# Part B of a two-branch attention kernel: dense Q, K and output projections, heads laid out through DRAM, and a queue order written by hand

## The chip, the cores and the metric

The kernel runs as one program on one core of a Trainium2 chip. The metric is the device time of one execution in microseconds, compared as the median of several runs. The engines named below are PE (matrix multiplication, with its weight loads PEld), ACT (ScalarE), DVE (VectorE), POOL (GpSimd) and SP (SyncE, which here only issues DMAs). ACT issues DMAs too, on a queue of its own.

## What is computed

Two attention branches read the same x (2048 tokens of 640) and are mixed by a gate.

```python
g = sigmoid((x * gate_w).sum(-1))
# A: 64 segments of 32 tokens; 8 memory rows are carried from segment to segment
h = concat(mem, x_segment)                       # 40 rows
q, k, v = h @ Wq, h @ Wk, h @ Wv                 # 32 heads of 192
o = softmax(mask(q k^T * 192**-0.5)) v @ Wo;  mem = o[:8];  a = o[8:]
# B: 32 heads of 20; each token sees itself and 7 earlier tokens, 2 apart
q, k, v = split(x @ wqkv)
b = softmax(q . k[t - 2w], w = 0..7) v[t - 2w] @ wo
out = g * a + (1 - g) * b
```

All tensors are bf16. The program does branch B first, then a prepass that projects the x rows which share a tile with memory rows, then the 64 segments of branch A in a recurrence, then a last stage.

## The kernel before

Branch B is the function `part_b`. It takes the 2048 tokens in blocks of 484 (four full blocks, b = 0 to 3, and a last one of 112), and the 32 heads in 8 groups of four (g = 0 to 7). One pair (b, g) is a step; there are 40.

Four heads of a group lie 32 rows apart, so that four small matmuls can sit in the four 32-row strips of PE. A head has 20 rows only. The weights of Q and K (`wqk`, names wq_pad and wk_pad) are therefore copied into tiles with 32 columns a head, of which 12 are zero, and the output weights (`wop`, name wo_pad) are loaded by four DMAs into 20 of each 32 partitions.

The pieces of part B, with their lines in the profile:

- `make_xT(b)` transposes 512 tokens of x into `xT` (L164), loads the next x tiles on ACT's queue (L118), computes the gate (L175 to L181), and on POOL packs rows for branch A (L185 to L190); SP stores them in `xh_dram` (L187).
- `make_v(b)` projects V for four sets of 128 keys (L213).
- `proj(b, g)` projects Q and K of one group of heads from the padded weights (L226), five matmuls each; DVE copies Q to SBUF, ACT copies K (helper lines L79 and L77).
- `scores(b, g)` has two halves of two heads each. Each half is 8 matmuls (L244), an exponential on ACT (L249, tile bP) and a multiplication by the band mask on DVE (L253).
- `values(b, g)` is called a step later. It multiplies bP by ones (sum, ps_bZ) and by V (ps_bO), 16 matmuls each in turn (L266); ACT takes logarithm and exponential for the reciprocal (L271, L272), and DVE writes the product to `OT` (L274), which is laid out like the padded heads.
- `out_tile(ti)` multiplies 128 tokens of `OT` by wo_pad, 8 terms for each of two halves (L282); ACT and DVE scale by 1 - g (L285, L287) and ACT's queue stores to `bsc_dram` (L289).

PSUM has two buffers for projections, transposes, V and output, two pairs for scores, and one each for sum and value. The steps are written in the order of the loop below, but the order of the instructions on each engine is chosen by a planner that moves instructions by their priority.

```python
for i, (b, g) in enumerate(steps):
    if g == 2 and b + 1 < S // 512: make_xT(b + 1)
    if g == 6 and i + 8 < len(steps): make_v(b + 1)
    if i + 1 < len(steps): proj(*steps[i + 1])
    scores(b, g)
    if i > 0: values(*steps[i - 1])
    if g >= 1 and b > 0 and 128 * (ti + 1) <= BQ * b: out_tile(ti); ti += 1
```

Beside part B the weights of branch A are loaded. They are cut into 80 slices of 384 KB. `load_early` (after the first xh store) loads 23 of them (N_EARLY) to stay in SBUF, and copies all 20 slices of Wo in DRAM into `wscr`, where a partition's part is contiguous (L385). 27 more (`late[0]`) are loaded when part B gives its SBUF free, others in the prepass and after it. Fourteen slices do not stay and are streamed once a segment (tile wst). The prepass projects Q, K (L442) and V (L454) and is held until the first xh store; the segment loop and the last stage are `part_a` and `part_z` (L569 and on).

Of the kernel before, what the change touches and what calls it, by code (L numbers as in the profile page):

```python
# [15 lines left out]
N_EARLY = 23  # L16
# [11 lines left out]
class _K:  # L28
# [61 lines left out]
    def part_b(self):  # L90
# [3 lines left out]
        BQ = 4 * NQ  # L94
        scale_b = 20.0 ** (-0.5)
# [6 lines left out]
        with ExitStack() as ctx:  # L102
# [13 lines left out]
            def load_x(i):  # L116
                xs[i] = io.tile([128, 640], BF, name="x_sb")
                nc.scalar.dma_start(xs[i][:], self.x2d[i * 128:(i + 1) * 128, :])  # L118
# [5 lines left out]
            wop = wp.tile([128, 8, 640], BF, name="wo_pad")  # L124
            wqk = [wp.tile([128, KC, 32, 32], BF, name=f"w{n}_pad") for n in "qk"]
            xT = wp.tile([128, KC, HALO + S], BF, name="xT")
            OT = wp.tile([128, 8, S], BF, name="OT")
            wsrc = self.wqkv.rearrange("(c p) f -> p c f", p=128)
            for n, w in enumerate(wqk):
                nc.gpsimd.memset(w[:, :, :, 20:32], 0.0)  # L130
                raw = OT[:].rearrange("p g t -> p (g t)")[:, 3200 * n:3200 * n + 3200]
                (nc.scalar, nc.sync)[n].dma_start(raw.rearrange("p (c f) -> p c f", c=KC), wsrc[:, :, 640 * n:640 * n + 640])
                for kc in range(KC):
                    eng = (nc.vector, nc.gpsimd)[(KC * n + kc) % 2]
                    eng.tensor_copy(w[:, kc, :, 0:20], raw[:, 640 * kc:640 * kc + 640].rearrange("p (h d) -> p h d", d=20))
            nc.sync.dma_start(gw[:], self.gate_w.rearrange("(c p o) -> p c o", p=128, o=1))
            nc.scalar.dma_start(wv[:], wsrc[:, :, 1280:1920])
            nc.gpsimd.memset(wop[:], 0.0)
            wosrc = self.wo.rearrange("(g h d) f -> h d g f", h=4, d=20)
            for hh in range(4):  # L140
                nc.sync.dma_start(wop[32 * hh:32 * hh + 20, :, :], wosrc[hh])
# [14 lines left out]
            self.g_sb = wp.tile([128, self.NT], F32, name="g_sb")  # L156
            self.omg_sb = wp.tile([128, self.NT], F32, name="omg_sb")

            def make_xT(b):
                t0 = 512 * b  # L160
                for kc in range(KC):
                    ps = bank(BF, "ps_xT")
                    for i in range(4):
                        nc.tensor.transpose(ps[:, i * 128:(i + 1) * 128], xs[4 * b + i][:, kc * 128:(kc + 1) * 128],  # L164
                                            self.ident[:])
                    self.evac(xT[:, kc, HALO + t0:HALO + t0 + 512], ps[:, 0:512])
# [5 lines left out]
                for i in range(4):  # L172
                    c0 = HALO + t0 + 128 * i
                    for kc in range(KC):
# [5 lines left out]
                nc.vector.reciprocal(self.g_sb[:, gs], gz[:, gs])  # L180
                nc.vector.tensor_scalar(out=self.omg_sb[:, gs], in0=self.g_sb[:, gs], scalar1=-1.0, scalar2=1.0,  # L181
# [5 lines left out]
                xh_store = nc.sync.dma_start(self.xh_dram[16 * b:16 * b + 16].rearrange("s p f -> p s f"),  # L187
                                    xh[:].rearrange("p s c t -> p s (c t)"))
                self.first_store = self.first_store or xh_store.ins
# [13 lines left out]
            def make_v(b):  # L203
                nq, nu, c0 = shape_of(b)
                nk = nq + 7
                for u in range(nu):
                    V = wk.tile([128, 652], BF, name=f"bV{u}")
                    nc.vector.memset(V[:, 640:652], 0.0)
                    k0 = c0 + 242 * (u // 2) + u % 2
                    for f in range(2):  # L210
                        ps = bank(F32, "ps_bv")
                        for kc in range(KC):
                            nc.tensor.matmul(ps[0:nk, 0:320], lhsT=xT[:, kc, k0:k0 + 2 * nk - 1:2],  # L213
                                             rhs=wv[:, kc, 320 * f:320 * f + 320], start=(kc == 0), stop=(kc == KC - 1))
                        self.evac(V[0:nk, 320 * f:320 * f + 320], ps[0:nk, 0:320])
                    Vs[b, u] = V

            qk = {}

            def proj(b, g):  # L220
                nq, nu, c0 = shape_of(b)
                nt = nq * nu
                for n, (o0, nn) in enumerate(((c0 + HALO, nt), (c0, nt + HALO))):
                    ps = bank(F32, "ps_bqk")
                    for kc in range(KC):
                        nc.tensor.matmul(ps[:, 0:nn], lhsT=wqk[n][:, kc, 4 * g:4 * g + 4, :].rearrange("p h d -> p (h d)"),  # L226
                                         rhs=xT[:, kc, o0:o0 + nn], start=(kc == 0), stop=(kc == KC - 1))
                    t = wk.tile([128, BQ + HALO], BF, name="b" + "qk"[n] + "T", bufs=3)
                    self.evac(t[:, 0:nn], ps[:, 0:nn], "dve" if n == 0 else "act")
                    qk[b, g, n] = t  # L230
# [3 lines left out]
            def scores(b, g):  # L234
# [61 lines left out]
            make_xT(0)  # L296
            with tc.issue_after(self.first_store):
                self.load_early()
            make_v(0)
            proj(*steps[0])  # L300
            ti = 0
            for i, (b, g) in enumerate(steps):
# [648 lines left out]
```

## Time and profile before

| | us |
|---|---|
| median of 3 runs | 1759.83 (1757.96 to 1762.52) |
| the profiled execution, its own time | 1748.09 |
| its span, first to last instruction | 1746.1 |
| part B with its start | 0 to 225.4 |
| prepass | 225.4 to 384.5 |
| 64 segments of branch A | 384.5 to 1687.2 |
| last stage | 1687.2 to 1746.1 |

Over the span PE is busy 1666.4 us (95%), ACT 868.5, DVE 649.4 and POOL 69.9. The granted clock of PE is 0.998. In a row of a profile, "L226 PE MATMUL ps_bqk<-xT,wk_pad 128*128 128x498 bf16 x160 | 38.8, 372 | 1.7 <-ACT" reads: line 226 of the kernel, engine and operation, output and inputs, shape, how many; busy time in us and mean ns of one; the idle time of the engine ahead of them, and what ended it. Matmuls are pipelined, so the mean of one is longer than the distance from one to the next.

### The profile page before, as it was taken

Reading aid. Unit: us, or ns where it says so; the run is one execution under the profiler, and the core shown is the slowest. Engines: PE = TensorE matmul, PEld = TensorE weight load, DVE = VectorE, ACT = ScalarE, POOL = GpSimd, SP = SyncE. Lnnn points to the kernel's source line nnn. Section 1 sums busy time; section 2 is a strip of 40 time slices with the busy share of each in tenths; the row PEclk is TensorE's granted clock in tenths of the full one; section 3 lists DMA queues with packets and bytes.
Section 4 is the critical chain, followed back from the end, with each engine's and each line's share of the span. In section 5 each row is a group of like instructions: output and inputs, shape, how many; then the busy total and the mean of one; then the engine's idle time right before and its main releaser. Section 6 shows DMA issues by size and latency. Waiting matters only on the chain.

```text
span 1746.1 us, 82407 instructions
## 1 busy us (share of the span) xinstructions
PE 1666.4 (95%) x36527; PEld 994.9 (57%) x36527; DVE 649.4 (37%) x2065; ACT 868.5 (50%) x2377; POOL 69.9 (4%) x132
## 2 busy tenths in 40 slices
PE   6899999999999999999999999999999999999989
PEld 3555544445556555556555555555555555555557
DVE  4565533223333333333333333333333333333330
ACT  3776632224555555555555555555555545555550
POOL 4011000000000000000000000000000000000000
PEclk9999999999999999999999999999999999999999
DMA  6951184899999999999999999999999989999981
GB/s 172 335 133 27 42 303 113 221 275 309 307 299 304 298 309 299 305 301 308 295 302 302 299 300 300 302 298 307 303 297 305 298 295 300 306 302 298 300 288 30
DMA packets 280648, 466.50 MB, mean 267 GB/s; under 512 B 94820, under 2 KB 155748, under 8 KB 280292
## 3 DMA queue, kind: packets, MB, share of 16 engines
q1 hardware_dynamic: 178632, 401.83, 69.6%
q10 hardware_dynamic: 101660, 59.41, 11.7%
q8 instruction: 285, 4.67, 1.1%
q14 instruction: 71, 0.58, 0.1%
HBM read 427.47 MB, written 41.55 MB: 269 GB/s over the span
## 4 chain that ended last, share of the span: by engine, by line
PE 86%; ACT 7%; issue 2%; DMA 2%; DVE 2%; ACTq 1%; DVEq 0%
PE ps_qk L569 26%; PE ps_v L662 13%; PE ps_wo L726 12%; PE ps_qkT L586 6%; PE ps_pre L442 6%; PE ps_S L616 5%; PE ps_oT L685 3%; PE ps_z L883 3%; PE ps_bqk L226 3%; ACT bP L249 2%; PE ps_pre L454 2%; ACT ZB L810 2%; PE ps_mem L736 1%; PE ps_bv L213 1%; PE ps_S L625 1%
## 5 line engine op out<-in xcount | busy, mean ns | idle before, releaser
L578 ACT CAST TZ<-ps_qk 128x384 bf16<-128x384 f32 x448 | 208.2, 479 | 326.2 <-PE ps_qk L569 180.4
L569 PEld LDWEIGHTS <-hT 128*32 128x32 bf16 x10240 | 246.5, 96 | 150.0 <-DVE hT L739 13.2
L593 DVE COPY ZB<-ps_qkT 128x384 bf16<-128x384 bf16 x256 | 91.6, 358 | 377.6 <-PE ps_qkT L586 211.7
L569 PE MATMUL ps_qk<-wres_q,hT 128*32 128x384 bf16 x4096 | 225.8, 327 | 1.8 <-issue 1.5
L662 PE MATMUL ps_v<-wlate_v,hT 128*32 128x384 bf16 x4096 | 224.6, 329 | 0.0
L726 PEld LDWEIGHTS <-TZ 128*32 128x32 bf16 x6144 | 153.6, 96 | 65.8 <-issue 18.0
L569 PE MATMUL ps_qk<-wlate_k,hT 128*32 128x384 bf16 x2560 | 159.7, 328 | 0.0
L569 PE MATMUL ps_qk<-wst,hT 128*32 128x384 bf16 x1792 | 153.2, 328 | 0.3 <-issue 0.2
L662 PEld LDWEIGHTS <-hT 128*32 128x32 bf16 x5120 | 113.6, 96 | 68.9 <-issue 6.2
L726 PE MATMUL ps_wo<-wlate_oa,TZ 128*32 128x384 bf16 x2560 | 139.2, 327 | 2.3 <-issue 2.3
L616 PE MATMUL ps_S<-ZB,TZ 128*128 128x160 bf16 (+1 forms) x1024 | 136.9, 238 | 0.4 <-issue 0.4
L586 PE MATMUL ps_qkT<-ident,TZ 128*128 128x128 bf16 x1536 | 130.2, 221 | 0.2 <-issue 0.2
L726 PE MATMUL ps_wo<-wlate_ob,TZ 128*32 128x256 bf16 x2688 | 123.2, 275 | 7.4 <-issue 7.3
L586 PEld LDWEIGHTS <-TZ 128*128 128x128 bf16 x1536 | 89.1, 98 | 61.3 <-issue 40.8
L569 PE MATMUL ps_qk<-wres_k,hT 128*32 128x384 bf16 x1792 | 120.3, 328 | 1.2 <-issue 0.6
L634 ACT ACTIVATE ZB<-ps_S 32x224 bf16<-32x224 f32 x256 | 89.0, 348 | 41.7 <-PE ps_S L625 38.1
L696 DVE CAST TZ<-ps_oT 128x192 bf16<-128x192 f32 x256 | 79.4, 351 | 63.6 <-PE ps_oT L690 63.6
L696 ACT CAST TZ<-ps_oT 128x192 bf16<-128x192 f32 x256 | 69.7, 327 | 57.7 <-PE ps_oT L690 57.7
L616 PEld LDWEIGHTS <-TZ 128*128 128x128 bf16 (+1 forms) x1024 | 58.9, 95 | 68.4 <-issue 41.0
L739 DVE CAST hT<-ps_mem 128x24 bf16<-128x24 f32 x126 | 22.6, 179 | 195.7 <-PE ps_mem L736 195.7
L669 ACT CAST TZ<-ps_v 128x384 bf16<-128x384 f32 x192 | 92.3, 481 | 3.2
L546 POOL COPY TZ<-ZB 128x384 bf16<-128x384 bf16 x64 | 32.5, 507 | 1495.9 <-DMA ZB<-zpk_dram 582.5
(142 smaller groups left out, 2431.2 us busy)
## 6 DMA issues: line engine op xcount, KB each, us to landing
wst<-in_A_Wq_dram SPq DMA_DIRECT2D x260, 384.0 KB
wst<-in_A_Wv_dram SPq DMA_DIRECT2D x260, 384.0 KB
wst<-in_A_Wk_dram SPq DMA_DIRECT2D x195, 384.0 KB
wst<-wscr SPq DMA_DIRECT2D x192, 384.0 KB
zpk_dram<-ZS ACTq DMA_DIRECT2D x4, 3072.0 KB
ZB<-zpk_dram ACTq DMA_DIRECT2D x64, 192.0 KB
wscr<-in_A_Wo_dram SPq DMA_DIRECT2D x20, 384.0 KB
wres_q<-in_A_Wq_dram SPq DMA_DIRECT2D x16, 384.0 KB
```

The costliest lines, as they stand in the source:

```text
L226: nc.tensor.matmul(ps[:, 0:nn], lhsT=wqk[n][:, kc, 4 * g:4 * g + 4, :].rearrange("p h d -> p (h d)"), rhs=xT[:, kc, o0:o0 + nn], start=(kc ...
L442: nc.tensor.matmul(ps[:], lhsT=sls[r][kc][:, c0:c0 + 128], rhs=zTi[:, kc, :], start=(kc == 0), stop=(kc == KC - 1))
L569: nc.tensor.matmul(pq[32 * j:32 * j + 32, 0:384], lhsT=hT[:, kc, :], rhs=sl[:, 384 * j:384 * j + 384], start=(kc == 0), stop=(kc == KC - 1 ...
L578: cp(sts[i], pqs[i][:, 0:384])
L586: nc.tensor.transpose(pT[:, t, :, :, :].rearrange("p j b i -> p (j b i)"), st[:, 128 * t:128 * t + 128], self.ident[:])
L593: nc.vector.tensor_copy(q_blocks(R)[:, 1:5, :, :].rearrange("p b c i -> p c b i"), pT.rearrange("p t j b i -> p (t j) b i"))
L616: nc.tensor.matmul(grid(h, par)[:, :, 0:80].rearrange("p j (b r i) -> p j b r i", r=2, i=8)[:, :, :, r, :], lhsT=KT[k0:k1, 12 * r + c:12 * ...
L634: nc.scalar.activation(E[ps], pSs[h][ps, :, 112 * j:112 * j + 112], ACT.Exp, scale=scale_a)
L662: nc.tensor.matmul(pvs[R][32 * j:32 * j + 32, 0:384], lhsT=hT[:, kc, :], rhs=sl[:, 384 * j:384 * j + 384], start=(kc == 0), stop=(kc == KC ...
L669: cp(V[R], pvs[R][:, 0:384])
L696: cps[j % 2](oTxs[2 * h + j // 2][:, 6 * (j % 2):6 * (j % 2) + 6, :], pos[j][:, 0:240].rearrange("p (c q) -> p c q", q=40)[:, :, 8:40])
L726: nc.tensor.matmul(pso[part][32 * jj:32 * jj + 32, 0:n], lhsT=oTxs[2 * (R // 2) + j // 2][:, 6 * (j % 2) + 3 * (R % 2) + t, :], rhs=o_weig ...
```

## The change

Q and K are projected densely, in five chunks of 128 columns a block instead of eight groups of four padded heads, and the output projection has five terms instead of eight. The rows of the heads are put 32 apart by DMA: each chunk is copied to a staging tile (`bqkD`, four buffers), stored in DRAM, and read back by halves of 16 heads into `bqkT`, four DMAs of 20 partitions each (`load_qk`). The normalized output goes the same way back: four DMAs of 20 partitions store it by halves in DRAM, and one loads it densely into `OT` (`load_o`). This is done a block ahead: while block b is attended, block b + 1 is projected.

The order on PE, ACT, DVE and SP is written out by hand (`manual_schedule`); each step has scores, the values of the step before, and a list of jobs. In `values` all 16 sums come before all 16 products. The last, short block is attended in two steps of 16 heads instead of eight of four. One early slice is loaded a step, 20 in all (N_EARLY), and only seven slices of Wo are copied to `wscr`; the other thirteen are read from Wo itself. The stores to `bsc_dram` go to SP's queue. The prepass is held until the output of block 2 is reloaded (`mid_load`). The zero padding, its memsets and copies are gone.

```diff
-N_EARLY = 23
+N_EARLY = 20
...
-                nc.scalar.dma_start(xs[i][:], self.x2d[i * 128:(i + 1) * 128, :])
+                eng = nc.sync if i < 2 else nc.scalar
+                eng.dma_start(xs[i][:], self.x2d[i * 128:(i + 1) * 128, :])
...
-            wop = wp.tile([128, 8, 640], BF, name="wo_pad")
-            wqk = [wp.tile([128, KC, 32, 32], BF, name=f"w{n}_pad") for n in "qk"]
+            wo = wp.tile([128, KC, 640], BF, name="b_wo")
+            wqk = [wp.tile([128, KC, 640], BF, name=f"b_w{n}") for n in "qk"]
...
-            OT = wp.tile([128, 8, S], BF, name="OT")
+            OT = wp.tile([128, KC, S], BF, name="OT")
...
-            for n, w in enumerate(wqk):
-                nc.gpsimd.memset(w[:, :, :, 20:32], 0.0)
...
-                    eng.tensor_copy(w[:, kc, :, 0:20], raw[:, 640 * kc:640 * kc + 640].rearrange("p (h d) -> p h d", d=20))
+            nc.sync.dma_start(wqk[0][:], wsrc[:, :, 0:640])
+            nc.scalar.dma_start(wqk[1][:], wsrc[:, :, 640:1280])
+            nc.sync.dma_start(wv[:], wsrc[:, :, 1280:1920])
...
+            def proj(b, f, n):
...
+                if n == 0:
+                    qk["D"] = wk.tile([128, 2, BQ + HALO], BF, name="bqkD", bufs=4)
+                t = qk["D"]
+                ps = bank(F32, "ps_bqk")
+                for kc in range(KC):
+                    nc.tensor.matmul(ps[:, 0:nn], lhsT=wqk[n][:, kc, 128 * f:128 * f + 128], rhs=xT[:, kc, c0:c0 + nn],
+                                     start=(kc == 0), stop=(kc == KC - 1))
+                self.evac(t[:, n, 0:nn], ps[:, 0:nn], "dve" if n == 0 else "act")
+                if n == 1:
+                    for half in range(2):
...
+                            nc.sync.dma_start(qk_dram[b][half, :, r0 - 320 * half:r1 - 320 * half, :].rearrange("n p x -> p n x"),
+                                              t[r0 - 128 * f:r1 - 128 * f, :, 0:nn])
+            def load_qk(b, half):
...
+                t = wk.tile([128, 2, 4, BQ + HALO], BF, name="bqkT", bufs=3)
+                src = qk_dram[b][half].rearrange("n (g h d) x -> h d (n g) x", h=4, d=20)
+                for hh in range(4):
+                    nc.sync.dma_start(t[32 * hh:32 * hh + 20, :, :, 0:nn].rearrange("p n g x -> p (n g) x"), src[hh])
...
+                if gs[-1] % 4 == 3:
+                    g = gs[-1]
+                    for hh in range(4):
+                        nc.sync.dma_start(heads(ot_dram[b][:])[hh][:, g - 3:g + 1, :], oT[32 * hh:32 * hh + 20, :, 0:nt])
+            def load_o(b):
...
+                load = nc.sync.dma_start(OT[:, :, BQ * b:BQ * b + nt], ot_dram[b][:].rearrange("(c p) n -> p c n", p=128))
+                if b == 2:
+                    self.mid_load = load.ins
...
+                for c in range(KC):
+                    nc.tensor.matmul(ps[:, 0:320], lhsT=OT[:, c, 128 * ti:128 * ti + 128],
+                                     rhs=wo[:, c, 320 * f:320 * f + 320], start=(c == 0), stop=(c == KC - 1))
...
+                for i, (b, gs) in enumerate(steps):
+                    g, nb, jobs = gs[0], b + 1, []
+                    if nb < NB:
+                        nu = shape_of(nb)[1]
+                        if g == 0 and nb < S // 512:
+                            jobs += [lambda kc=kc: xT_chain(nb, kc) for kc in range(KC)] + [lambda: gate(nb)]
+                        chunk = {1: 0, 2: 1, 3: 2, 5: 3, 6: 4}.get(g)
+                        if chunk is not None:
+                            jobs += [lambda n=n: proj(nb, chunk, n) for n in range(2)]
+                        vs = {1: (0,), 2: (1,), 3: (2,), 4: (3, 4), 7: (5, 6, 7)}.get(g, ())
+                        jobs += [lambda u=u: v_chain(nb, u // 2, u % 2) for u in vs if u < 2 * nu]
+                        for _ in range({0: 1, 4: 2, 5: 1, 6: 1, 7: 2}.get(g, 0) if b < NB - 2 else 1):
+                            if outs:
+                                jobs.append(outs.pop(0))
...
+                    scores(b, gs, 0)
+                    scores(b, gs, 1)
+                    if prev:
+                        values(*prev)
+                    mask(b, gs, 0)
+                    if jobs:
+                        jobs.pop(0)()
+                    mask(b, gs, 1)
+                    if prev:
+                        recip(*prev)
+                    if jobs:
+                        jobs.pop(0)()
+                    if prev:
+                        norm(*prev)
+                    for job in jobs:
+                        job()
...
+                    if nb < NB and g == 4:
+                        load_qk(nb, 0)
+                    if nb < NB and g == 7:
+                        load_qk(nb, 1)
+                    if g == 1 and b > 0:
+                        add_outs(b - 1)
+                    if early:
+                        early.pop(0)()
...
-        so = [k for k in self.slice_keys() if k[0] in ("oa", "ob") and k not in self.early]
+        so = [k for k in self.slice_keys() if k[0] in ("oa", "ob") and (k in self.stream_keys or k in self.late[3])]
...
-        with tc.issue_after(k.first_store):
+        with tc.issue_after(k.mid_load):
             k.prepass()
```

310 lines of the change are left out of this document (179 added, 131 removed).

## The prediction

> **What bounds the kernel now.** First the busy time of each engine in the stretches of the program (columns: stretch, its length, busy time of PE, PEld, DVE, ACT and POOL with instruction counts, granted clock, DMA share, GB/s): part B with start, then prepass, segment loop and last rows.
>
> ```profile
> 0.00:225.40 225.40, 193.27 (x2724) 113.79 (x2724) 124.46 (x251) 138.80 (x249) 37.49 (x68) 0.99 0.46 138
> 225.40:384.50 159.10, 156.22 (x724) 70.42 (x728) 47.98 (x71) 40.57 (x72) 0.51 (x1) 1.00 0.78 234
> 384.50:1687.20 1302.70, 1264.23 (x31540) 766.65 (x31543) 469.20 (x1730) 677.85 (x2048) 31.95 (x63) 1.00 0.92 302
> 1687.20:1746.10 58.90, 52.73 (x1552) 44.00 (x1544) 7.75 (x15) 11.28 (x10) 0.00 (x0) 1.00 0.26 76
> ```
>
> PE fills the prepass and the segment loop, and the change leaves their arithmetic alone. What it can win lies in the first 225.4 us. The same view by block of part B (start, blocks 0 to 3, short block 4):
>
> ```profile
> 0.00:31.40 31.40, 17.62 (x100) 10.09 (x100) 13.12 (x36) 5.49 (x10) 16.41 (x19) 0.95 0.66 184
> 31.40:64.20 32.80, 30.82 (x455) 16.98 (x454) 19.76 (x36) 24.69 (x40) 3.66 (x3) 1.00 0.81 293
> 64.20:111.00 46.80, 41.09 (x593) 23.84 (x592) 25.68 (x49) 31.56 (x52) 4.25 (x3) 1.00 0.93 258
> 111.00:158.00 47.00, 42.56 (x606) 25.13 (x606) 27.62 (x50) 30.80 (x51) 13.17 (x43) 1.00 0.12 31
> 158.00:198.00 40.00, 35.69 (x518) 20.20 (x520) 23.09 (x39) 27.33 (x45) 0.00 (x0) 1.00 0.09 28
> 198.00:225.40 27.40, 25.50 (x464) 17.56 (x464) 15.19 (x44) 18.93 (x56) 0.00 (x0) 1.00 0.11 40
> ```
>
> A full block takes 47 us: PE 41 to 43, ACT 31. PE is the bound, ACT has a third to spare. Which PE work, by groups with shapes apart, over part B:
>
> ```profile
> L249 ACT ACTIVATE bP<-ps_bS 128x968 bf16<-128x968 f32 x64 | 59.5, 984 | 0.1
> L226 PE MATMUL ps_bqk<-xT,wk_pad 128*128 128x498 bf16 x160 | 38.8, 372 | 1.7 <-ACT gz_sb L178 1.7
> L282 PE MATMUL ps_bo<-wo_pad,OT 128*128 128x320 bf16 x256 | 38.7, 300 | 0.7 <-DVE bqT L79 0.7
> L226 PE MATMUL ps_bqk<-xT,wq_pad 128*128 128x484 bf16 x160 | 38.0, 367 | 4.6 <-ACT bo L285 4.5
> L213 PE MATMUL ps_bv<-wv_sb,xT 128*128 128x320 bf16 x160 | 27.3, 331 | 4.7 <-DVE bV L79 3.3 <-ACT bV L77 1.4
> ```
>
> Then one step without extra work, in the timeline: ACT runs from the two exponentials through logarithm and reciprocal to the next K copy without a gap, so beneath PE's load ACT is the second bound.
>
> ```profile
> 68.75 1.85 ACT L249 ACTIVATE bP<-ps_bS 128x968 bf16<-128x968 f32 x2
> 70.48 0.59 ACT L271 ACTIVATE b_rz<-ps_bZ 128x484 f32<-128x484 f32 x1
> 71.11 0.61 ACT L272 ACTIVATE b_rz<-b_rz 128x484 f32<-128x484 f32 x1
> 71.62 0.57 ACT L77 CAST bkT<-ps_bqk 128x498 bf16<-128x498 f32 x1
> ```
>
> Last, what DMA moves of the kinds that the change adds: 23 to 25 us is the padded Wo load (DMAs of 20 partitions), 26 to 28 the xh store (320 B runs), 45 to 60 slices in 3 KB rows, 70 to 80 mostly the Wo copies in 768 B rows.
>
> ```profile
> 23.00:25.00 2.00, 2.00 (x10) 1.09 (x9) 0.49 (x1) 0.00 (x0) 0.17 (x1) 0.50 0.69 123
> 26.00:28.00 2.00, 2.00 (x14) 1.14 (x12) 0.69 (x2) 0.42 (x1) 0.61 (x2) 0.94 1.08 210
> 45.00:60.00 15.00, 13.86 (x194) 8.08 (x191) 8.96 (x16) 11.13 (x19) 0.00 (x0) 1.00 1.03 404
> 70.00:80.00 10.00, 8.76 (x161) 5.75 (x160) 6.90 (x15) 8.79 (x14) 0.46 (x1) 1.00 0.98 291
> ```
>
> **PE per block.** Prices from the chain of waits: 20 projection matmuls in 4.21 us (0.21 each), 30 V matmuls in 4.36 (0.145), 16 output matmuls in 2.17 to 2.33 (0.14); scores plus values of a step take 0.91 to 1.15 in the timeline, say 1.0. A full block now: 80 projections 16.8, V 5.8, 64 output 9.0, eight steps 8, transposes and gate about 2: 41.6, against 41.1 read. After: dense Q and K need 5 chunks of 128 columns instead of 8 groups, 50 matmuls of 498 (10.5); output 5 terms instead of 8, 40 matmuls (5.6); the rest as before: 31.9. That removes 30 and 24 matmuls a block. Over the kernel 150 and 96 matmuls with as many weight loads, 492 PE instructions, and the built program has 72,564 instead of 73,056: the change does what it says. Scores on 20 rows instead of 32 I cost at nothing, since the columns are the same.
>
> **ACT per block.** Exponentials, logarithm and reciprocal: 68.75 to 71.62 is 2.87 a step, 23 a block. Copies after: K 5 x 0.57 (8 before), V 4 x 0.43, output 4 x 0.52, xT 2.5 x 0.59: 31. Four x loads in two of the blocks cost ACT 0.44 each to issue (1.33 for three at 13.9 us), 1.8; the 16 stores of bsc (0.33 each) move to SP. So PE and ACT come level at 32 to 33.
>
> **The written order.** On PE each step is scores, values of the step before, then the jobs. Walking steps through the queues with these rows: a step with two projections and a V or output chain is 3.8 on PE against 3.4 to 3.8 on ACT. The step with the transposes costs 5.2 to 7.0, because its five copies queue behind the exponentials and only two PSUM buffers feed them, and the x loads sit in ACT's queue before the gate. Sum for a block 31 (block 0, no output), 35 and 34.5. Block 3 has little projection: ACT's 27.2, so 28.
>
> **DMA per block.** New are Q and K stores of 1.28 MB and loads of the same, heads out 0.62 and back 0.62, beside eight early slices 3.15, x and xh 0.66 each, bsc 0.6: 8.9 MB. The head loads and head stores are DMAs of 20 partitions: 1.9 MB at 123 GB/s is 15.4 us. Slices 3.15 MB at 404: 7.8. xh at 210: 3.1. The other 3.15 MB in rows of about 1 KB at 291 to 395: 8 to 11. Sum 34 to 37, as long as the block. The share of 0.69 at 23 to 25 us says that some 11 of the 16 engines were busy under such DMAs, so other traffic may partly slip beside them: bounds 21 (wholly beside) to 37. [...]
>
> So I take 37.5 for blocks 1 and 2, between the walk's 35 and a queue that is full, 33 for block 0, 28.5 for block 3. Heads are loaded about three steps ahead (11 us); four loads of a half at 123 GB/s land in 5 to 7 us, so they arrive unless the queue is backed up by 5 us. SP runs in the written order and each of its DMAs waits for the one eight earlier on its semaphore; a store that waits for a copy holds back the early slices and head loads behind it, all needed steps later.
>
> **Start.** Gone: pad copies and memsets on POOL and DVE (PE waited 2.7 for an xT copy on DVE behind them). Added before the first score: all ten projection chains. x blocks 2 and 3 now stand behind the 0.8 MB of K weights, landing near 10.3 instead of 8.5; transposes done at 13, projections to 24.8 (10.5 plus 1.2 of waiting on ACT's x loads and the gate), V to 30.6; the first heads, issued near 23.8, land near 31. First score at 31.5, as before (31.4). Bounds 28 to 35.
>
> **End.** The two steps of block 4: ACT 2.8 and 1.7 after a load that may be 0.5 late, mask 0.7, values, logarithm, reciprocal and product 2.7; then store and reload, each some 3 (a 20-partition DMA issued at 20.30 released its lane by 24.19), under ten output chains of 0.7; last tile 1.4. About 17 from its first exponential.
>
> **Sum.** 31.5 + 33 + 37.5 + 37.5 + 28.5 + 17 = 185, against 225.4: 40.4 less.
>
> **Prepass and loop.** Three slices fewer early: 2.9 us more DMA (0.97 each), due only 52 us after part B ends (PE's two q passes before it; 120 such matmuls take 26.07 in the chain), so nothing; 2.9 without that cover. Stream loads now wait for the third output load, still 30 us before use: nothing. Thirteen Wo slices come straight in 768 and 512 B rows: 1.35 instead of 0.97 each by 291 and 404 GB/s, 5 us of DMA, mostly where DMA was full (share 1.0 from 350 to 375), with a share of 0.6 after it, ahead of a 3.1 us wait of PE for a streamed V slice in segment 0. Bounds -3 to +5; I take +1, since the slack behind it is 4 us. In total -39.4: the profiled 1748.1 (span 1746.1, 2.0 around it) becomes 1708.7. That run lies 11.7 below the median; on the median it is 1759.8 - 39.4 = 1720.
>
> **Rivals.** (a) The head DMAs slip beside the rest: blocks at the walk, start 31, end 16: 31 + 31 + 35 + 34.5 + 28 + 16 = 175.5, so 1711. For it: share 0.69. Chance 0.17. (b) The engines that carry the heads bind and the waits add bubbles: blocks 38, 44, 44, 30, sum 204.5, so 1740. For it: the DMA sum of 37 without a gap. Chance 0.19. (c) Slower: all goes through SP's one queue, eight DMAs in flight, 36 a block; if a DMA takes L to land, a block takes 36 L / 8. Beyond L = 8 us that sets the block. The gain of 39.4 is spent at 13 more on each of blocks 0 to 2 (mean 36), 49 us, L = 10.9. For it: 18 Wo copies went out in 28.7 us, 1.6 each, or 12.8 to land eight deep. Against: only eight DMAs of a block are that large; eight of the mean 0.25 MB at 291 GB/s are 7 us. At 12.8 a block is 57.6: 1785. Chance 0.08. (d) As (c) with L near 10.9: within 0.3%, 5.3 us, about what a measurement of this kernel can tell from no change. Chance 0.03.
>
> **Numbers.** My forecast, 1712 to 1731, has 0.53. The range of 1705 to 1743 takes in (a) and (b) and leaves (c), (d) and some edges out. Faster 0.89, same 0.03, slower 0.08.
>
> **What would show it.** The first score near 31.5; starts of blocks 33 to 38 apart; PE's stall there on ACT, or on the loads into bqkT if (b); prepass from about 185; segment loop unchanged in length. I am wrong if PE waits for bqkT for more than 5 us a block, if DMA share is below 0.7 in blocks 1 and 2 while they still take over 40, or if the loop grows.

## The result, and the profile after

The changed kernel takes 1741.8 us against 1760.1 for the kernel before (medians of four runs each): a ratio of 0.9896, interval 0.9879 to 0.9913, 18.3 us less. In a second comparison the ratio was 0.9881 (0.9858 to 0.9905). The forecast was 1720, 39.4 less. The sign and the range held; the gain is less than half of the forecast.

First the stretches of the program in the profile after (columns as before): part B, prepass, segment loop, last stage.

```profile
0.00:210.20 210.20, 160.60 (x2478) 94.41 (x2479) 107.19 (x213) 130.98 (x210) 28.94 (x60) 0.89 0.74 191
210.20:369.50 159.30, 155.43 (x709) 70.40 (x728) 48.08 (x71) 40.82 (x72) 0.51 (x1) 1.00 0.82 247
369.50:1678.70 1309.20, 1266.18 (x31544) 766.21 (x31544) 469.01 (x1730) 677.97 (x2048) 32.09 (x63) 1.00 0.92 300
1678.70:1739.30 60.60, 54.38 (x1552) 47.50 (x1540) 7.70 (x15) 11.33 (x10) 0.00 (x0) 0.97 0.28 82
```

Part B ends at 210.2 instead of 225.4. PE works 33 us less in it, but at a mean clock of 0.89 instead of 0.99, so the work removed, priced at full clock, was larger still; half of what was freed is idle time. Now the blocks, each from its first exponential (start, blocks 0 to 3, end):

```profile
0.00:30.10 30.10, 21.43 (x138) 11.76 (x138) 7.35 (x23) 7.69 (x15) 5.09 (x11) 1.00 0.69 198
30.10:62.90 32.80, 29.85 (x482) 16.86 (x482) 21.79 (x41) 27.22 (x44) 4.17 (x3) 0.90 0.88 215
62.90:105.90 43.00, 34.51 (x560) 20.00 (x564) 24.53 (x47) 30.45 (x48) 4.18 (x3) 0.92 0.86 229
105.90:142.20 36.30, 32.90 (x550) 19.26 (x553) 25.54 (x54) 29.67 (x47) 15.49 (x43) 0.95 0.88 222
142.20:180.30 38.10, 24.90 (x521) 16.18 (x524) 19.44 (x37) 26.18 (x43) 0.00 (x0) 0.87 0.63 166
180.30:210.20 29.90, 17.02 (x250) 10.36 (x250) 8.54 (x14) 9.78 (x17) 0.00 (x0) 0.66 0.45 97
```

Block 0 and block 2 are as forecast. Block 1, block 3 and the end are not: 5.5, 9.6 and 12.9 us too long, 28 together, more than the 25.2 us by which part B missed the forecast of 185. The group of the output projection shows why (busy and mean, then idle time before it), and the list of PE's waits up to 212 us names the transfers:

```profile
L345 PE MATMUL ps_bo<-b_wo,OT 128*128 128x320 bf16 x160 | 30.9, 343 | 20.5 <-DMA OT<-bo_dram 18.4 <-ACT bV L77 0.7 <-DVE bqkD L79 0.6
```

```profile
PE ps_bo L345 <- DMA OT<-bo_dram: 18.4, 3, 8.3
PE ps_bS L260 <- DMA bqkT<-bqk_dram: 5.9, 4, 4.4
```

The output projection of block b - 1 runs in the steps of block b, and its input OT now comes back through DRAM. Three times PE stood before it, in block 1, block 3 and the end; PE runs in the written order, so the next scores stood behind it (in block 1 the two chains of the output at 89.0, the scores at 91.78). SP's queue in block 1 (time of issue, its length, line, DMA) shows where the reload was:

```profile
72.92 4.59 SPq L328 DMA_DIRECT2D bo_dram<-boT  x4
77.61 0.39 SPq L186 DMA_DIRECT2D xh_dram<-xh_blk  x1
78.06 2.80 SPq L527 DMA_DIRECT2D wres_q<-in_A_Wq_dram  x1
80.98 0.37 SPq L234 DMA_DIRECT2D bqk_dram<-bqkD  x1
81.93 0.37 SPq L333 DMA_DIRECT2D OT<-bo_dram  x1
```

The stores are out by 77.5, the reload stands behind an xh store, a slice and a head store, goes out at 81.93 and is used at 89.0. The stores were late themselves: DVE had finished block 0's last product at 67.85, but SP had a head load to issue first, at 67.45, and then stood 1.9 us ahead of a slice and 5.0 us ahead of the stores, which the profile puts down to earlier DMAs. So ten of the fourteen us from the product to the reload had passed when the stores were out. In block 3 it is the gate's own trip through DRAM that stands ahead of it: SP issues the gate store at 148.73 and the reload of it at 153.83, and nothing between.

```profile
148.73 0.94 SPq L375 DMA_DIRECT2D g_dram<-g_sb  x1
153.83 0.78 SPq L377 DMA_DIRECT2D gA<-g_dram  x2
...
155.70 0.39 SPq L333 DMA_DIRECT2D OT<-bo_dram  x1
```

At the end two more trips follow one another: block 3's last stores go out from 188.52, its reload at 194.79, block 4's at 201.31. PE waits 4.39 us for the last heads and 4.68 us, until 199.51, for the reload, and then has ten output chains of five matmuls still to do:

```profile
185.98 0.25 PE L260 MATMUL ps_bS<-bqkT 20*63 20x56 bf16 x1 [4.39 <-DMA bqkT<-bqk_dram]
191.98 2.85 PE L345 MATMUL ps_bo<-b_wo,OT 128*128 128x320 bf16 x10
199.51 4.97 PE L345 MATMUL ps_bo<-b_wo,OT 128*128 128x320 bf16 x20 [4.68 <-DMA OT<-bo_dram]
204.83 4.60 PE L345 MATMUL ps_bo<-b_wo,OT 128*128 128x320 bf16 x30 [0.36 <-ACT bo L348]
```

Last, a cost that no step of the prediction had: granted clock. Below are the stretch that begins within the 8.3 us stall, and most of the end:

```profile
156.00:166.20 10.20, 5.25 (x68) 3.38 (x68) 1.73 (x4) 3.59 (x6) 0.00 (x0) 0.50 0.78 203
183.30:203.80 20.50, 11.03 (x187) 6.82 (x188) 4.22 (x7) 4.91 (x8) 0.00 (x0) 0.50 0.55 107
```

With 33.1 to 39.9, 87.7 to 94.5 and 111.6 to 115.0 that makes 47.7 us of part B at half clock, with 31.5 us of PE work in them; in part B of the kernel before there was one such stretch of 3.4 us in the first profile, and 10.2 us of them in the second. The stretches in the changed kernel are 3.4, 6.8, 10.2 and 20.5 us long, each at 0.50. Three of them begin within PE's waits of 5.4, 8.3 and 4.4 us; the other two do not: 33.1 to 39.9 came with no PE gap over 0.5 us since 8.5, and 111.6 to 115.0 with none over 1.1 us since 94.5. Both come at the transposes of x, and PE was busy for 2.18 and 1.91 of the 3.4 us ahead of them.

### The profile page after: what moved, and what is told of

Same layout as the page of the kernel before. It is cut to its first block, busy times and chain, and to the rows that moved or that the text cites. A ratio compares the mean times of both kernels' runs of the same rounds, so it can differ in the third digit from the quotient of the medians.

```text
span 1739.3 us, 82027 instructions
## 1 busy us (share of the span) xinstructions
PE 1636.6 (94%) x36266; PEld 978.5 (56%) x36281; DVE 632.0 (36%) x2027; ACT 861.1 (50%) x2338; POOL 61.5 (4%) x124
## 4 chain that ended last, share of the span: by engine, by line
PE 85%; DMA 6%; ACT 4%; issue 3%; SPq 1%; DVE 1%; ACTq 1%; DVEq 0%
PE ps_qk L699 26%; PE ps_v L792 13%; PE ps_wo L856 12%; PE ps_pre L572 6%; PE ps_qkT L716 6%; PE ps_S L746 5%; PE ps_oT L815 3%; PE ps_z L1013 3%; PE ps_pre L584 2%; PE ps_bqk L227 2%; ACT ZB L940 2%; PE ps_mem L866 1%; DMA bqkT<-bqk_dram 1%; PE ps_S L755 1%; DMA OT<-bo_dram 1%
## 5 line engine op out<-in xcount | busy, mean ns | idle before, releaser
L699 PE MATMUL ps_qk<-wlate_k,hT 128*32 128x384 bf16 x3328 | 202.1, 328 | 0.0
L792 PE MATMUL ps_v<-wst,hT 128*32 128x384 bf16 x1024 | 86.9, 329 | 6.2 <-DMA wst<-in_A_Wv_dram 6.2
L764 ACT ACTIVATE TZ<-ps_S 32x224 bf16<-32x224 f32 x256 | 88.8, 347 | 2.3
```

Of the source, the lines that this page charges most:

```text
L699: nc.tensor.matmul(pq[32 * j:32 * j + 32, 0:384], lhsT=hT[:, kc, :], rhs=sl[:, 384 * j:384 * j + 384], start=(kc == 0), stop=(kc == KC - 1 ...
L764: nc.scalar.activation(E[ps], pSs[h][ps, :, 112 * j:112 * j + 112], ACT.Exp, scale=scale_a)
L792: nc.tensor.matmul(pvs[R][32 * j:32 * j + 32, 0:384], lhsT=hT[:, kc, :], rhs=sl[:, 384 * j:384 * j + 384], start=(kc == 0), stop=(kc == KC ...
```

## Experiments

Lengths of blocks below are taken as above; "prepass start" is the end of part B.

**Is the difference outside part B real?** The kernel before, unchanged, profiled again:

> The kernel before, profiled a second time, to learn how far its segment loop differs from one execution to the next: its profiled run was 11.7 us below the median of its runs, and the loop of the changed kernel was 6.5 us longer than that one's. If the loop's length is a property of the kernel, it is again 1302.7 within 1.5 us and the change costs 6.5 us there. If it is chance (each of 63 segments takes 19.70 us or up to 1.9 more), this execution's loop is anywhere from 1302 to 1316.

Measured: part B to 228.6, the loop, from its first to its last memory update, 1265.9 instead of 1253.3; this execution took 1764.8. Over all twenty profiles of this study the loop lies anywhere between 1253 and 1267, whatever the kernel. So it is chance as far as the kernels go (what moves it is not known), and the 11.7 us by which the first profile lay below its median were mostly this. The changed kernel again:

> The changed kernel a second time, unchanged. If its part B is a property of the program, the prepass starts at 210.2 within 2 us and the three waits for the output reload are there again (18.4 us within 3); its loop lies anywhere between 1253 and 1267; ratio 0.988 to 0.991.

The prepass started at 212.3, the waits for OT were 19.4 us in three stalls, the loop took 1261.6 as in its first profile, and the ratio was 0.9881. So the change moves part B by some 16 us (225.4 and 228.6 against 210.2 and 212.3). From the prepass start to the first memory update it is 184.3 to 185.0 against 183.8 to 184.4, and after the last one 82.4 to 83.1 against 83.5 to 83.8. The remaining 3 us of the medians' 18 to 19 are below what the loop scatters.

**The reload, undone three ways.** First its place on SP:

```diff
+                    if g == 0 and b > 0:     # behind norm(*prev)
+                        load_o(b - 1)
...
-                def add_outs(b):             # was: end of step 1
-                    load_o(b)
```

> The reload of a block's normalised heads (OT, 605 KB) is issued right behind the stores it reads, at the end of step 0 of the next block, instead of at the end of step 1 behind the xh store, two early slices, head stores and, in block 3, the gate loads. Theory A (SP's written order holds the reload back): block 1's reload goes out near 79.5 instead of 81.9, block 3's near 150.5 instead of 155.7, the last near 191.5 instead of 194.8; PE's wait for OT (18.4 us in three stalls) falls to 6 to 9 and the prepass starts at 196 to 201 instead of 210.2, the time falls to 1728 to 1733. Theory B (the DMA engines are full, the reload lands when the bytes before it are through): the waits stay at 15 or more and the prepass starts within 3 us of 210. Rival C: SP now waits for the stores to land with the next block's head stores behind it, and the wait moves to bqkT: OT below 9, bqkT above 5.9 by as much.

The reload went out at 79.39, block 1 had no wait for it and fell from 43.0 to 36.8, block 3 from 38.1 to 34.7. But prepass start was 211.5 and the ratio 0.9905 (0.9886 to 0.9924), as before the edit:

```profile
63.80:100.60 36.80, 34.22 (x543) 19.89 (x543) 24.34 (x47) 30.07 (x48) 4.17 (x3) 0.91 0.85 217
174.30:211.50 37.20, 18.67 (x268) 11.45 (x269) 8.42 (x14) 9.78 (x16) 0.00 (x0) 0.63 0.45 105
```

What the blocks gave, block 2 (39.0) and the end (37.2 instead of 29.9) took: at the end PE waited 7.4 us for bqkT, and 5.7 for OT. So rival C holds for the whole, and theory A only inside blocks 1 and 3. Nor is SP's order the whole trip: with nothing between, the reload still went out 2.4, 7.7 and 4.8 us after the last store in blocks 1, 2 and 3 (4.4, 7.2 and 7.8 in the changed kernel), and the profile puts that wait down to the landing of the stores. Second, the bytes, taken away:

```diff
-                    if early:
-                        early.pop(0)()
```

> The 27 early slices and Wo copies (10.6 MB) are taken out of part B's steps and issued after its last step, so only part B is read (the prepass must then wait for its weights). Theory A (order and round trips): the slices cost SP some 0.5 us each and little else; PE's wait for OT stays above 12 of 18.4 us, blocks 1 and 3 above 40 and 36 us. Theory B (bytes): with 3.15 of 8.9 MB a block gone, OT lands in time in block 1 (wait below 1 us there instead of 5.4) and block 1 falls from 43 to 36; block 3, where the DMA share was 0.24 to 0.27 during the wait, keeps its 8.3 in either theory.

This is one execution, and its total of 1761.5 us cannot be compared, since the weights came late and part B ended at 231.3. Block 1 took 36.8 with no wait for OT, block 3 35.4 with 5.8. So the slices, too, are able to make block 1's reload late, but the first run shows that their bytes need not: there all of them were in. The more telling number is that with 3.15 MB less and a DMA share of 0.57 to 0.61, blocks 1 and 2 take 36.8 and 36.2, no less than with all slices (36.8 in the run before, 36.3 in the changed kernel), and that PE waited for no DMA in either. So in these two blocks DMA does not set the length. Third, no reload to wait for:

```diff
-                    nc.tensor.matmul(ps[:, 0:320], lhsT=OT[:, c, 128 * ti:128 * ti + 128],
+                    nc.tensor.matmul(ps[:, 0:320], lhsT=xT[:, c, 128 * ti:128 * ti + 128],
```

> The output projection multiplies the transposed x, which is in SBUF since long, instead of the reloaded heads: same matmuls, same stores and reloads, but no matmul waits for a reload (the heads are left out of part B's output). Theory A (the reload wait is the term that was mis-sized): the 18.4 us of waits go, and with them the stretches at half clock behind them, some 6 us more: block 1 falls from 43.0 to 36, block 3 from 38.1 to 29, the end from 29.9 to 22 to 24; the prepass starts at 184 to 189, time 1716 to 1721. Rival B (the queue is full, another transfer is late next): PE waits for bqkT 10 us or more instead of 5.9 and the prepass starts after 198. Rival C (ACT and PE carry their work more slowly than priced): no wait above 3 us, yet blocks 1 and 3 stay above 40 and 34.

The blocks took 32.7, 35.2, 38.1 and 29.2; blocks 1 and 3:

```profile
63.50:98.70 35.20, 31.85 (x543) 18.89 (x543) 24.53 (x47) 30.27 (x49) 4.18 (x3) 1.00 0.91 241
136.80:166.00 29.20, 22.21 (x495) 14.74 (x492) 19.41 (x37) 26.05 (x43) 0.00 (x0) 1.00 0.62 156
```

So the excess of blocks 1 and 3 is the reload and the half clock behind it. But the end took 38.4, with 7.3 us for bqkT and 9.3 for the output tile, whose stores stand on SP behind the last reload. The prepass started at 204.4, neither near 186 nor at 210; the ratio was 0.9865 (0.9838 to 0.9893).

**The end, one link at a time.** Heads of the last block earlier:

```diff
+                        chunk = {0: 0, 1: 1, 2: 2, 3: 3, 4: 4}.get(g) if last else {1: 0, 2: 1, 3: 2, 5: 3, 6: 4}.get(g)
...
+                    if nb < NB and g == (3 if last else 4):
+                    if nb < NB and g == (5 if last else 7):
```

> The last block's Q and K projections go in steps 0 to 4 of block 3 instead of 1, 2, 3, 5, 6, and its head loads are issued at the end of steps 3 and 5 instead of 4 and 7. Theory A (the heads' way through DRAM had two short steps to go, and each stall halves the clock behind it): the 4.4 us wait for bqkT before step 33 goes, the end falls from 29.9 to 23 to 26, the prepass starts at 203 to 207, time 1734 to 1738. Rival B (the end hangs on the outputs' way through DRAM, load of block 3's heads behind the stores, whatever the scores do): PE's wait for OT grows by what bqkT gives back, prepass start 208 or later.

The waits for bqkT fell to 1.1 us in all, the waits for OT grew to 21.3, and the prepass started at 211.2, ratio 0.9908 (0.9888 to 0.9927): rival B. The small DMAs later:

```diff
-                    if b >= 3:
-                        for load in misc[:3]: ...
```

> The 31 small DMAs on SP (gates out and back, first segment's x and memory) are issued after the last step instead of three a step from block 3 on. Theory A (in SP's written order the gate reload, which waits 4.2 us for the gate store, holds block 3's reload of heads back, and three more such DMAs a step cost SP 1.9 us): block 3's reload goes out near 151 instead of 155.7, the last two near 191 and 198 instead of 194.8 and 201.3; OT waits of 8.3 and 4.7 fall to 4 and 2, prepass start 200 to 204. Rival B (they only move): the 31 DMAs, 0.65 us each, stand ahead of the prepass's streamed weights, and the prepass, 159.3 now, grows by what part B gives back.

Block 3 took 35.0 and its stall fell from 8.3 to 5.5 us: its reload went out at 153.62, still 5.4 us after the stores, when these had landed, so only some 3 us of that stall were the gate's. The reloads at the end went out at 184.94 and 192.13, nine to ten us sooner. But the 31 DMAs now stood ahead of the output stores, part B ended at 223.5, and the ratio was 0.9973 (0.9956 to 0.9989). Not the prepass paid, as rival B had it, but the end itself, in one wait of PE:

```profile
PE ps_bo L345 <- ACT bo L348: 20.9, 1, 20.9
```

The clock, kept up with matmuls in the gaps:

```diff
+                    if i == len(steps) - 1: filler(16)   # 128x484, read by nobody
...
+                    if n == len(outs) - 8: filler(24)
```

> PE gets matmuls that nobody reads where it stood still at the end: 16 of 484 columns ahead of the last step's scores (3.4 us at 0.21 each, the wait there was 4.4) and 24 ahead of the output chains that wait for block 3's reload (5.0, the wait there was 4.7 and earlier work ran at half clock). Nothing else changes. Theory A (the stalls put the clock to a half, and work at half clock is a cost beside the wait): the half-clock stretch from 183.3 to 203.8 (11 us of PE work in it) goes or shrinks to under 7 us, the prepass starts at 204 to 207 instead of 210.2. Rival B (at the end everything waits for landings): prepass start within 1.5 us of 210, clock or not.

From 183.3 to 203.8 the mean clock was 0.92 instead of 0.50, and the prepass began at 209.9, ratio 0.9926 (0.9897 to 0.9954): rival B. At this end, where landings set the pace, the half clock cost nothing that shows.

Eight short steps at the end, as before:

```diff
-                steps += [(NB - 1, tuple(range(4 * n, 4 * n + 4))) for n in range(2)]
+                steps += [(NB - 1, (g,)) for g in range(8)]
```

> The short last block goes in eight steps of one head group again instead of two steps of four. Theory A (fewer, larger instructions are what the two steps win): ACT has 16 exponentials and 16 logarithms and reciprocals on 56 to 112 columns instead of 4 and 4, some 10 us instead of 5.6, the prepass starts 3 to 5 us later (213 to 215), time 1745. Rival B (the end is set by the round trips of the heads, and six more steps are cover for them): PE's wait of 4.4 us for the second half's heads goes, the end stays within 1.5 us of 29.9.

The end took 41.2, prepass start 219.6, ratio 0.9995 (0.9974 to 1.0017). The wait for bqkT at the end fell to 2.2, but the six steps more put the end of part B 7 to 9 us later (than 212.3 and 210.2), not 3 to 5. By the ratio the whole gain is gone, some 17 to 20 us; part B accounts for 7 to 9 of them, and the rest is not explained.

**The Wo copies.** All twenty again:

```diff
-        so = [k for k in ... if k[0] in ("oa", "ob") and (k in self.stream_keys or k in self.late[3])]
+        so = [k for k in ... if k[0] in ("oa", "ob")]
```

> All 20 Wo slices are copied to scratch rows again instead of the 7 that are streamed or loaded last: 13 copies more, 384 KB each, 5.1 MB or 17 us of DMA at 291 GB/s, one a step behind the 27 early slices, the last 6 after part B. Theory A (part B's stalls come from order and round trips, and the prepass has 52 us of slack): blocks 0 to 2 as they are, block 3 and the end within 2 us, the loop within its scatter of 1253 to 1267: time within 0.3% of 1742. Theory B (bytes count): part B ends 3 to 6 us later, time 1745 to 1748. Theory C (straight Wo rows of 768 and 512 B cost the prepass or the loop): up to 5 us less, 1737.

The ratio was 1.0016 (0.9997 to 1.0036): the whole gain was gone. No block changed by more than 2 us; the end took 47.1, and SP's queue shows why: the copies that are left over, then the output stores.

```profile
207.71 0.38 SPq L333 DMA_DIRECT2D OT<-bo_dram  x1
208.14 6.09 SPq L513 DMA_DIRECT2D wscr<-in_A_Wo_dram  x6
214.33 13.38 SPq L352 DMA_DIRECT2D bsc_dram<-bo  x6
```

Order or bytes? The same with two a step, so that none is left:

```diff
-                    if early:
-                        early.pop(0)()
+                    for load in early[:2]: load()
+                    del early[:2]
```

> All 20 Wo slices copied, as in the run whose part B ended at 227.5, but two slices or copies a step instead of one, so that all are out by the middle of block 2 and none stands ahead of the last output stores on SP. Theory A (order: the 6 copies left over were what held the last stores back): blocks 0 to 3 within 3 us of the changed kernel's, prepass start at 208 to 214, time 1740 to 1746. Theory B (bytes: 8.9 MB a block fill the engines, and 3.1 MB more a block come on top): blocks 0 and 1 grow by 6 to 11 us each, prepass start at 222 or later.

The end was 28.4 again, but blocks 1 and 2 took 44.9 and 44.2, prepass start 217.7, ratio 0.9927 (0.9903 to 0.9951). Some ten of the 17 us were order at the end; seven came back in block 2, whose reload was now late as well (four stalls, 23.6 us). And the part alone, on the kernel before:

> The kernel before with one part of the change alone: 7 Wo slices copied to scratch rows instead of 18, the other 11 read straight from Wo when they are needed. Theory A (in the old order the copies ran beside blocks that PE bound: block 1 with a DMA share of 0.93 took 46.8 and block 2 with 0.12 took 47.0): part B ends within 1.5 us of 225 to 229, time within 0.3% of the kernel before. Theory B (the copies' 4.3 MB are what the change's gain came from): part B ends 10 us or more earlier, ratio 0.993 or less. Theory C (straight rows of 768 and 512 B cost the prepass or the loop): ratio 1.002 to 1.006.

(The profile counts 20 copies before and 7 here, 13 fewer, not 11.) Part B ended at 225.9 and the ratio was 0.9981 (0.9962 to 0.9999): theory A, with some 3 us, at most 7. In the old order the copies cost next to nothing. In the new one, at one DMA a step, keeping them costs the whole gain, and at two a step a part of it.

**Staging.** Two buffers instead of four (`name="bqkD", bufs=2`):

> Two staging buffers for the dense Q and K instead of four. A chunk's copies must then wait until the store of the chunk before the last has landed. Theory A (a step takes 3.8 us and a store lands in 3 to 4, so it has landed two chunks later): blocks 0 to 3 unchanged, start 0 to 2 later, time within 0.3% of 1742. Theory B (the store waits in SP's order behind slices and other stores, and the copies in ACT's and DVE's order behind it): PE waits for the copies 1 to 2 us a chunk, part B ends 10 to 25 us later, 1752 to 1767.

The prepass started at 216.1, ratio 0.9929 (0.9902 to 0.9957): 4 to 6 us later, between the theories. PE waited 8.5 us for K's staging copy, 2.8 at once in block 0 and 5.0 in block 1; the start was 1.4 later.

**All links together.** The reload behind its stores, the last block's heads early, the 31 DMAs behind the last output stores, block 2's output chains from step 4 of block 3 on, three output tiles:

```diff
-for _ in range({0: 1, 4: 2, 5: 1, 6: 1, 7: 2}.get(g, 0) if b < NB - 2 else 1):
+for _ in range({0: 1, 4: 2, 5: 1, 6: 1, 7: 2}.get(g, 0) if b < NB - 2 else (1 if g >= 4 else 0)):
...
-                for load in early + misc: load()
-                for job in outs: job()
+                for load in early: load()
+                for job in outs: job()
+                for load in misc: load()
```

> Four edits together: the reload right behind its stores; the last block's projections in steps 0 to 4; the 31 small DMAs behind the last output stores; in block 3 the output chains of block 2 from step 4 on, so that some are left to fill the wait for block 3's reload; and a third buffer for the output tile. Theory A (what each gave alone was lost again because the next link in the end's chain of landings was late; with all links moved the sum shows): blocks 33, 36.5, 37 to 39, 30 and an end of 22 to 24, prepass start at 190 to 197, time 1722 to 1729. Rival B (the wait moves again, to SP, which now stands still for each reload's stores): prepass start at 203 or later, time 1735 or more. Rival C: part B as in A, but the 31 DMAs on SP hold back the prepass's streams, prepass start to the first memory update longer than 184.9.

The prepass started at 196.1, with one wait of 0.6 us for OT; the blocks took 33.3, 37.6, 38.6 and 28.1, the end 27.5. The ratio was 0.9842 (0.9817 to 0.9866). From the prepass start to the first memory update it is 186.3, and 185.7 in the repeated run below, against 184.3 and 185.0 in the changed kernel, so rival C is worth 2 us at most. The same kernel again:

> The combined kernel unchanged, a second time: prepass start 196 within 2 us, no wait for the output reload above 1 us, ratio to before between 0.982 and 0.987.

The prepass started at 194.2, with one wait of 1.5 for OT; the time was 1729.1 against 1759.5, ratio 0.9820 (0.9792 to 0.9849). This version beats both kernels; the changed one stood at 0.9881 and 0.9896. Its block 3 and end:

```profile
137.90:165.60 27.70, 21.24 (x495) 14.28 (x493) 18.04 (x35) 25.23 (x42) 0.00 (x0) 0.94 0.74 186
165.60:194.20 28.60, 19.26 (x271) 12.14 (x271) 9.83 (x17) 10.90 (x19) 0.00 (x0) 0.82 0.59 172
```

The same with no reload to wait for:

> The same with the output projection on the transposed x, so that no matmul waits for a reload (heads left out of part B's output): the floor that the sum of prices in the prediction stood for. Theory A (the prices of PE and ACT were right, only waits were missing): blocks 33, 36, 37, 29, end 18 to 20, prepass start at 184 to 188. Rival B (some 10 us of it are neither reload nor head waits): prepass start after 194.

The prepass started at 195.2, the end took 28.4 and the ratio was 0.9821 (0.9798 to 0.9844), no better: rival B. What is left of the end in the repeated run is 7.7 us of two steps, 14.8 of output chains (16 of them) and 4.7 in which PE waits for output tiles whose stores stand on SP behind the last reload. Two attempts at it gave nothing. Heads ahead of the stores in each step, and three output chains less at the end:

```diff
+                    if nb < NB and g == (3 if last else 4): load_qk(nb, 0)   # ahead of norm(*prev)
...
-(1 if g >= 4 else 0)
+{4: 1, 5: 2, 6: 2, 7: 2}.get(g, 0)
```

> The combined kernel with two more edits: a block's head loads are issued ahead of the stores of the normalised heads in the same step, and seven of block 2's output chains instead of four go in block 3, three less in the end. Theory A (each link moved shows now): the 3.5 us of waits for heads at the start of block 2 go to under 1, the end of 27.5 falls to 23 to 25, prepass start at 188 to 193, ratio to before 0.979 to 0.983. Rival B (SP stands still for the landing of the last head store before the load, and the time is given back there): prepass start within 2 us of 196.

The prepass started at 197.3, ratio 0.9857 (0.9833 to 0.9880): block 2 fell to 37.3 and the end to 25.3, but block 3, with three chains more, took 35.3 instead of 28, and PE waited 4.7 for OT again. And the clock, where nothing was thought to land:

```diff
+                    if i >= 29: filler(12 if i == len(steps) - 1 else 4)
```

> The combined kernel with matmuls that nobody reads, 484 columns each: 4 ahead of the scores of the last four steps but one, 12 ahead of the last step's scores, 28 in all, 6 us of PE work at full clock in a stretch where PE stood idle between steps. Theory A (the half-clock stretch from 167.9 to 184.9 is what the gaps bring, and the output chains in it are PE bound): the stretch goes or shrinks below 7 us, the chains before 184.9 take 0.75 instead of 1.3 each, the prepass starts 2 to 5 us earlier, at 191 to 194. Rival B (the chains wait for landings there too, or the added work costs what the clock gives): prepass start at 195 or later.

The clock was 1.00 from 164 to 176 and 0.60 to 0.83 after it, and the prepass started at 198.6: rival B. Its ratio of 0.9821 (0.9789 to 0.9853) is that of the kernel without the filling.

## Why the prediction was right or wrong

**Prices: right.** PE's 31.9 for a full block at full clock: block 1 of the run without reload waits has 31.85 us of PE at clock 1.00. ACT's 31 to 33 came out a little lower, at 29.7 to 30.5. Scores on 20 rows cost no more than on 32: 15.8 us for 512 matmuls against 16.1. Part B has 246 matmuls fewer in the profile (2478 against 2724), as said.

**Start and blocks 0 and 2: right in size.** First score at 29.6 (forecast 31.5), blocks 32.8 and 36.3 (33 and 37.5). But the reason given for 37.5, "a queue that is full", fell: without the slices blocks 1 and 2 are as long, with no wait of PE for a DMA. That leaves the written order on PE and ACT, which the walk put at 35 and 34.5; no run isolates it, but that sum was the better one, and the DMA sum of 34 to 37 only happened to lie beside it. With it falls the weight that the prediction gave to DMAs of 20 partitions, put at some 11 of the 16 engines, an estimate from the share of 0.69 at 23 to 25 us. Whether so many were full no run shows, since a mean share of 0.57 to 0.61 over the 16, without slices, would allow it; but PE did not wait for such a DMA in these blocks.

**Blocks 1 and 3: the step that failed.** "SP runs in the written order and each of its DMAs waits for the one eight earlier on its semaphore; a store that waits for a copy holds back the early slices and head loads behind it, all needed steps later." Such waits are in both profiles: in the kernel before, the slices issued at 47.28, 48.26 and 49.23 went out within 0.02 us of the landing of the DMA eight earlier on SP (issued at 43.34, 43.76 and 44.22), and in the changed kernel SP stood 1.9 and 5.0 us for earlier DMAs in block 1. I walked this queue for the heads and not for the output's reload, which is needed in the third step after its issue in block 1 and in the next one in block 3, and stands behind the landing of its own stores, and on SP behind other stores, slices and the gate's trip. The forecast cost of that reload was nothing; it was 13.7 us of stalls in the two blocks and made them 15 us longer (43.0 + 38.1 against 37.5 + 28.5). With it removed block 3 took 29.2, and 27.7 in the combined kernel: the 28.5 was a good price for the work.

**The end: 17 forecast, 29.9 measured.** "Then store and reload, each some 3 ..., under ten output chains of 0.7." The chains were put under the wrong trip. Eight of those ten wait for block 3's own reload, which is issued in the last step too, so that only two chains stood beside the wait. And a trip was mis-sized: from the first store of block 3's last half to the first use it took 11 us (188.5 to 199.5), not 6. The load "0.5 late" was 4.4. By the profile: 6.8 to the second step, 12.4 to the reload, 10.7 for ten chains. Moving single links did not help, since the next was as late; moving four took the end's start from 180.3 to 168.6 and 165.6 and left its length at 27.5 to 28.6.

**Clock: no term.** I took matmul prices from a trace with a clock of 0.99. Part B had 47.7 us at half clock, of which 37.5 came with stalls of 4 us and more. At the end this cost nothing that shows (the filled run); in blocks 1 and 3 it comes with the stall, and what part of the 15 us is clock was not separated.

**Prepass and loop: +1, right within the scatter.** My sign of being wrong, "the loop grows", was not usable: the loop scatters by 13 us. The other two signs (bqkT above 5 us a block, DMA share below 0.7 in blocks over 40) did not show either, since both asked about the heads.

**Rivals.** (b) named 1740, near the result, by another mechanism: "the engines that carry the heads bind", blocks 38, 44, 44, 30. The heads' loads cost PE 5.9 us in all, 4.4 of it at the end. (c) had the right place, SP's one queue, and the wrong price: not its throughput but single round trips in it. The profile also counts 20 Wo copies where (c) counts 18.

**What I costed at nothing.** Few Wo copies: next to nothing on the kernel before; 15 to 17 us of part B in the new order, where one DMA a step leaves six of them ahead of the last stores. Two last steps instead of eight: I gave it no term of its own, and it is worth 7 to 9 in part B.

## What to carry to other kernels

When data takes a trip through DRAM inside a hand-written order, write down for each trip the issue of the store, what stands on the queue up to the reload, the landing and the first use, and count it in steps of the consumer: the trips here took 11 to 16 us, three to four steps of 3.8. Do this for every trip and not only for the new ones that look large, and look for DMAs that wait themselves (a gate's store and reload) on the same queue. One late link hides the next: judge a fix by the sum of the waits after it, and expect a single edit to return little.

## What the runs showed of the hardware

In the changed kernel, stretches of 6.8 to 20.5 us with a granted clock of 0.50 came with PE's stalls of 4.4 to 8.3 us, and a chain of five output matmuls in them took 1.5 us instead of 0.85. Half clock also came without such a stall, at 33.1 and 111.6 us, where PE was busy 2.18 and 1.91 of the 3.4 us before, in a step with transposes.

The reloads through DRAM waited for their stores to land, and that time differed much: with nothing between them on SP, in the run with the reload moved, the reload of a full block's heads went out 2.4, 7.7 and 4.8 us after the last store's issue ended. In the changed kernel its 605 KB were in use 4.7 to 7.1 us after its issue, in the three places where PE stood waiting for it.
